# A decode step of attention over a 256 MiB cache: blocks of 8 MiB in three buffers in place of 2 MiB in eight

## The chip, the cores and the metric

The kernel runs on one core of one Trainium2 chip. The metric is device microseconds of one execution. The kernel before has 788.67 us as the median of 3 runs (788.57 to 788.68).

## What is computed

A token each of two sequences goes through grouped-query attention over a cache and, side by side, through a two-layer network. Everything is float32.

```
xn  = layernorm(x)                                   # x: [2, 1, 1024]
q   = (xn @ wq) as [2, 32 heads, 1, 128]             # wq: [1024, 4096]
k,v = k_cache, v_cache                               # each [2, 4 kv heads, 32768, 128]; 8 q heads share one
p   = softmax(q k^T / sqrt(128)) over 32768 positions
a   = (p v) @ wo                                     # wo: [4096, 1024]
m   = silu(xn @ w1) @ w2                             # w1: [1024, 3584], w2: [3584, 1024]
out = x + a + m
```

K and V are 128 MiB each, wq and wo 16 MiB each, w1 and w2 14 MiB each: 316 MiB are read once.

## The kernel before

All large operands come as blocks of 2 MiB, laid out on the host so that each of 128 partitions gets one contiguous row of 16 KiB (`W = 4096` columns). The helper `block` (L35) takes a tile from the pool `stream`, which has 8 buffers (L30), and issues its transfer on SP's queue (L40). SP issues in program order; a transfer into a buffer waits until the last reader of the block that was there has finished. So the order of the blocks in the program is the order of the stream, and up to eight blocks are queued or held.

All matmuls go through the helper `mm` (L44), so the profile gives L44 for each of them and the tile's name tells them apart. TensorE works in four column groups of 32: a matmul with 32 columns of weights writes partitions 32 g to 32 g + 31 of its output. The profile counts two instructions for each matmul.

The program's order is this. `queries(0)` (L108) projects xn with two blocks of wq to the eight queries of kv head 0; `project` (L92) is eight matmuls into `proj`, a copy on ScalarE (L99) and four small products. `mlp_in` (L114) does the same with seven blocks of w1 and keeps silu of the result in `hT`. Then for each kv head h, `queries(h)` for h > 0, `attention(h, b)` for both sequences, and two blocks of wo into the accumulator `acc` (L103). At the end seven blocks of w2 go into `acc`. The last of them is cut: three transfers of 1024 columns (512 KiB, rows of 4 KiB) and four of 256 columns (128 KiB, rows of 1 KiB), so that little work is left behind the last one. ScalarE copies `acc` (L205) and two transfers write the output (L207).

`attention` has two halves. For each of eight K blocks, the scores of 32 query columns (8 heads, the other 24 columns are zero) with 512 positions per column group go to `ps` (a PSUM tile of 128 x 1024, two buffers, L32). VectorE transposes it in 32 x 32 squares to `st` (L140), so that positions lie on partitions and a quarter of the columns is of use, and takes the maximum (L141). After the eighth block the maximum over all partitions is made by two small matmuls (`rm`, `gm`, `gd`, `gmax`, L145 to L155). Then, for each of eight V blocks, VectorE subtracts the maximum (L162), ScalarE takes the exponential (L163), VectorE sums it (`ls`, L164), and eight matmuls with the weights `e` as stationary operand add to `po`. The sum over partitions (`lsum`, L170), its reciprocal and the product with `po` give the head's output in `oT` (L181).

Of the kernel before, what the change touches and what calls it, by code (L numbers as in the profile page):

```python
# [8 lines left out]
F32 = mybir.dt.float32  # L9
AF = mybir.ActivationFunctionType  # L10
# [16 lines left out]
def gqa_plus_mlp_kernel(ctx: ExitStack, tc: tile.TileContext, x, kt, v, wq, wo, w1, w2, out):  # L27
    nc = tc.nc
    const = ctx.enter_context(tc.tile_pool(name="const", bufs=1))
    stream = ctx.enter_context(tc.tile_pool(name="stream", bufs=8))  # L30
    work = ctx.enter_context(tc.tile_pool(name="work", bufs=2))
    ps_s = ctx.enter_context(tc.tile_pool(name="ps_s", bufs=2, space=bass.MemoryType.PSUM))  # L32
    ps_1 = ctx.enter_context(tc.tile_pool(name="ps_1", bufs=1, space=bass.MemoryType.PSUM))

    def block(src, parts=1, first=0):  # L35
        """A streamed block: its first columns in transfers of a row tile, the others in parts."""
        t = stream.tile([P, W], F32, name="blk")
        cuts = [*range(0, first, D), *range(first, W, W // parts), W]
        for lo, hi in zip(cuts, cuts[1:]):
            nc.sync.dma_start(t[:, lo:hi], src[:, lo:hi])  # L40
        return t
# [4 lines left out]
    # ---- constants; sel[p, m] = 1 where p % 32 == m  # L46
    xt = const.tile([B, D], F32, name="xt")
    nc.scalar.dma_start(xt, x)
# [8 lines left out]
    qT = [const.tile([P, B, 32], F32, name=f"qT{i}") for i in range(2)]  # L57
    oT = [const.tile([P, REP, 32], F32, name=f"oT{i}") for i in range(2)]
    hT = const.tile([P, F // P, 32], F32, name="hT")
    xres = const.tile([P, QW], F32, name="xres")  # L60
    for t in (*qT, *oT, hT, xres):
        nc.gpsimd.memset(t, 0.0)
# [18 lines left out]
    xn = const.tile([B, D], F32, name="xn")  # L81
    nc.vector.tensor_scalar(xn, xt, mv[:, 0:1], rstd, op0=ALU.subtract, op1=ALU.mult)
    px = ps_1.tile([P, KT, B], F32, name="small")
    for k in range(KT):
        mm(px[:, k, :], xn[:, k * P:(k + 1) * P], ident[:B, :B])
# [6 lines left out]
    def project(w, o, n):  # L92
# [5 lines left out]
        pr = work.tile([P, 512], F32, name="pr")  # L98
        nc.scalar.copy(pr, pp)  # L99
        for i in range(n):  # L100
            mm(o[:, i, :], pr[:, i * P:(i + 1) * P], sel[:, :B])

    def accumulate(lhsT, w, start, stop):  # L103
        """acc[32 j + b, n] += lhsT[:, b] . w[:, j * 256 + n]"""
        for j in range(4):
            mm(acc[32 * j:32 * j + 32, :], lhsT, w[:, j * QW:(j + 1) * QW], start, stop)

    def queries(h):  # L108
        pq = ps_1.tile([P, REP, B], F32, name="small")
        for n in range(2):  # L110
            project(block(wq[2 * h + n]), pq[:, 4 * n:4 * n + 4, :], 4)
        nc.vector.tensor_copy(qT[h % 2][:, :, :REP], pq.rearrange("p h b -> p b h"))  # L112

    def mlp_in():  # L114
        pre = const.tile([P, F // P, B], F32, name="pre")
        for n in range(N1):
            ph = ps_1.tile([P, 4, B], F32, name="small")
            project(block(w1[n]), ph, 4)
            nc.vector.tensor_copy(pre[:, 4 * n:4 * n + 4, :], ph)
        e = const.tile([P, F // P, B], F32, name="sig")  # L120
        nc.scalar.activation(e, pre, AF.Exp, scale=-1.0)
        nc.vector.tensor_scalar_add(e, e, 1.0)
        r = const.tile([P, F // P, B], F32, name="rsig")
        nc.vector.reciprocal(r, e)
        nc.vector.tensor_mul(hT[:, :, :B], pre, r)

    def attention(h, b):
        q = qT[h % 2][:, b, :]
        # scores, transposed: partition 32 g + i holds positions 512 (4 a + g) + 32 j + i of each block
        s = []  # L130
        mx = work.tile([P, NC, REP], F32, name="mx")
        for c in range(NC):
            kc = block(kt[b, h, c])
            ps = ps_s.tile([P, 1024], F32, name="ps")
            for a in range(2):
                for g in range(4):
                    mm(ps[32 * g:32 * g + 32, a * 512:(a + 1) * 512], q,
                       kc[:, (4 * a + g) * 512:(4 * a + g + 1) * 512])
            st = work.tile([P, 32, 32], F32, name="st", bufs=NC + 1)
            nc.vector.transpose(st.rearrange("p j m -> p (j m)"), ps)  # L140
# [16 lines left out]
        ls = work.tile([P, NC, REP], F32, name="ls")  # L157
        po = ps_1.tile([P, 512], F32, name="po")
        for c in range(NC):
            vc = block(v[b, h, c])  # L160
            e = work.tile([P, 32, REP], F32, name="e", bufs=4)
            nc.vector.tensor_sub(e, s[c][:, :, :REP], gmax.to_broadcast([P, 32, REP]))  # L162
            nc.scalar.activation(e, e, AF.Exp, scale=SCALE)  # L163
            nc.vector.tensor_reduce(ls[:, c, :], e.rearrange("p j m -> p m j"), AX.X, ALU.add)  # L164
# [11 lines left out]
        ob = work.tile([P, 512], F32, name="ob")  # L176
        nc.scalar.copy(ob, po)  # L177
        pt = ps_1.tile([P, REP], F32, name="small")
        for j in range(4):
            mm(pt, ob[:, j * P:(j + 1) * P], sel[:, REP * j:REP * (j + 1)], j == 0, j == 3)  # L180
        nc.vector.tensor_mul(oT[h % 2][:, :, b], pt, rl)  # L181
# [12 lines left out]
    for n in range(N1):  # L194
        last = n == N1 - 1
        w = block(w2[n], 16 if last else 1, first=3 * D if last else 0)
        for i in range(3 if last else 4):
            accumulate(hT[:, 4 * n + i, :], w[:, i * D:(i + 1) * D], False, False)
    f = QW // 4
    for u in range(4):  # L200
        for j in range(4):
            mm(acc[32 * j:32 * j + 32, u * f:(u + 1) * f], hT[:, F // P - 1, :],
               w[:, 3 * D + (4 * u + j) * f:3 * D + (4 * u + j + 1) * f], False, u == 3)
# [33 lines left out]
```

## Time and profile before

| what | us or share |
|---|---|
| median of 3 runs | 788.67 us |
| span of the profiled execution, first to last instruction | 786.9 us |
| mean granted TensorE clock | 0.761 |
| PE busy | 482.1 us, 61% |
| VectorE (DVE) busy | 198.5 us, 25% |
| ScalarE (ACT) busy | 42.2 us, 5% |
| mean rate of the transfers over the span | 422 GB/s |

The page is of one profiled execution. Its rows name the source line, the engine, the operation and the tiles (`out<-in`), then the number of instructions, their busy time, the mean of one, and the idle time of the engine ahead of them with what ended it. "SPq" is the queue on which SP issues transfers, "PEld" the loading of weights into TensorE. In the chain of waits a row is start, length and what ran or was waited for; it is followed back from the last instruction. A transfer's row there runs from its issue to its landing.

### The profile page before, as it was taken

Reading aid. Unit: us, or ns where it says so; the run is one execution under the profiler, and the core shown is the slowest. Engines: PE = TensorE matmul, PEld = TensorE weight load, DVE = VectorE, ACT = ScalarE, POOL = GpSimd, SP = SyncE. Lnnn points to the kernel's source line nnn. Section 1 sums busy time; section 2 is a strip of 40 time slices with the busy share of each in tenths; the row PEclk is TensorE's granted clock in tenths of the full one; section 3 lists DMA queues with packets and bytes.
Section 4 is the critical chain, followed back from the end, with each engine's and each line's share of the span. In section 5 each row is a group of like instructions: output and inputs, shape, how many; then the busy total and the mean of one; then the engine's idle time right before and its main releaser. Section 6 shows DMA issues by size and latency. Waiting matters only on the chain.

```text
span 786.9 us, 7170 instructions
## 1 busy us (share of the span) xinstructions
PE 482.1 (61%) x3048; PEld 139.7 (18%) x3048; DVE 198.5 (25%) x340; ACT 42.2 (5%) x92; POOL 2.4 (0%) x12
## 2 busy tenths in 40 slices
PE   5776666565765566555565565556576565556655
PEld 3331111111221112111221111111131111111122
DVE  2013521342013420443003521352004420333000
ACT  1110000000000000001000000000000010001000
POOL 1000000000000000000000000000000000000000
PEclk9876676868587776978877869776857778857788
DMA  9999999999999999999999999999999999999996
GB/s 375 426 426 428 426 429 426 426 426 426 426 428 427 427 426 427 429 426 425 427 426 427 426 426 426 427 428 428 428 426 424 427 426 428 426 428 429 426 426 273
DMA packets 23682, 331.83 MB, mean 422 GB/s; under 512 B 2642, under 2 KB 3170, under 8 KB 3556
## 3 DMA queue, kind: packets, MB, share of 16 engines
q1 hardware_dynamic: 23624, 331.36, 99.3%
q8 instruction: 24, 0.39, 0.2%
q14 instruction: 6, 0.05, 0.0%
q10 hardware_dynamic: 28, 0.02, 0.0%
HBM read 331.37 MB, written 0.01 MB: 421 GB/s over the span
## 4 chain that ended last, share of the span: by engine, by line
DMA 87%; PE 11%; DVE 1%; issue 0%; ACT 0%; SPq 0%; ACTq 0%
DMA blk<-in_kt 37%; DMA blk<-in_v 33%; DMA blk<-in_w 12%; DMA blk<-in_wq 5%; PE po L44 4%; PE ps L44 3%; PE proj L44 2%; PE small L44 1%; PE acc L44 1%; DVE st L140 0%; SPq L40 0%; ACT pr L99 0%; ACT ob L177 0%; DVE mx L141 0%; DVE e L162 0%
## 5 line engine op out<-in xcount | busy, mean ns | idle before, releaser
L44 PE MATMUL ps<-blk,qT 128*32 128x512 f32 x1024 | 172.1, 805 | 115.0 <-DMA blk<-in_kt 97.7
L44 PE MATMUL po<-blk,e 128*32 128x512 f32 x1024 | 181.0, 849 | 92.5 <-DMA blk<-in_v 82.7
L140 DVE STREAM_TRANSPOSE st<-ps 128x1024 f32<-128x1024 f32 x64 | 80.0, 1250 | 179.5 <-PE ps L44 179.3
L44 PEld LDWEIGHTS ps<-blk,qT 128*32 128x32 f32 x1024 | 37.0, 129 | 241.6 <-issue 147.1
L44 PEld LDWEIGHTS po<-blk,e 128*32 128x32 f32 x1024 | 38.7, 137 | 214.9 <-issue 175.8
L163 ACT ACTIVATE e<-e 128x256 f32<-128x256 f32 x64 | 25.4, 417 | 438.0 <-DVE e L162 438.0
L44 PE MATMUL proj<-blk,xnT 128*32 128x512 f32 x240 | 43.5, 846 | 8.5 <-DMA blk<-in_wq 6.7
L162 DVE TENSOR_TENSOR e<-st,gmax 128x256 f32<-128x256 f32 x64 | 25.7, 422 | 65.2 <-PE po L44 64.7
L164 DVE TENSOR_REDUCE ls<-e 128x8 f32<-128x256 f32 x64 | 38.0, 615 | 13.1 <-ACT e L163 13.0
L181 DVE TENSOR_TENSOR oT<-small,rl 128x8 f32<-128x8 f32 x8 | 1.4, 172 | 157.9 <-PE small L44 157.9
L141 DVE TENSOR_REDUCE mx<-st 128x8 f32<-128x256 f32 x64 | 37.4, 585 | 2.2
L44 PE MATMUL acc<-blk,oT 128*32 128x256 f32 x256 | 25.1, 558 | 10.1 <-DMA blk<-in_wo 9.3
L44 PE MATMUL acc<-blk,hT 128*32 128x256 f32 (+1 forms) x248 | 18.1, 433 | 13.4 <-DMA blk<-in_w 13.2
L44 PE MATMUL small<-sel,pr 128*128 128x2 f32 x120 | 19.1, 281 | 11.0 <-ACT pr L99 11.0
L44 PEld LDWEIGHTS small<-sel,pr 128*128 128x128 f32 x120 | 17.8, 227 | 30.7 <-ACT pr L99 30.7
L112 DVE COPY qT<-small 128x16 f32<-128x16 f32 x4 | 0.7, 174 | 73.1 <-PE small L44 73.1
L44 PE MATMUL small<-ident,rm 128*8 128x128 f32 x16 | 3.5, 306 | 18.2 <-DVE rm L145 18.2
L99 ACT COPY pr<-proj 128x512 f32<-128x512 f32 x15 | 8.8, 585 | 103.2 <-PE proj L44 103.2
L44 PEld LDWEIGHTS acc<-blk,oT 128*32 128x32 f32 x256 | 10.2, 147 | 22.1 <-DMA blk<-in_wo 11.6
L44 PE MATMUL small<-lsum,ones 128*128 128x8 f32 x16 | 3.5, 293 | 15.9 <-DVE lsum L170 15.9
L177 ACT COPY ob<-po 128x512 f32<-128x512 f32 x8 | 4.7, 585 | 156.7 <-PE po L44 156.7
L44 PEld LDWEIGHTS proj<-blk,xnT 128*32 128x32 f32 x240 | 8.5, 135 | 25.6 <-issue 17.1
(49 smaller groups left out, 71.1 us busy)
## 6 DMA issues: line engine op xcount, KB each, us to landing
blk<-in_kt SPq DMA_DIRECT2D x64, 2048.0 KB, 36.2
blk<-in_v SPq DMA_DIRECT2D x64, 2048.0 KB, 36.0
blk<-in_w SPq DMA_DIRECT2D x13, 2048.0 KB, 30.6
blk<-in_wq SPq DMA_DIRECT2D x8, 2048.0 KB, 37.1
blk<-in_wo SPq DMA_DIRECT2D x8, 2048.0 KB, 35.9
blk<-in_w SPq DMA_DIRECT2D x3, 512.0 KB, 30.1
blk<-in_w SPq DMA_DIRECT2D x4, 128.0 KB, 12.4
xres<-in_x ACTq DMA_DIRECT2D x2, 4.0 KB
```

What stands on the lines that cost most here:

```text
L44: nc.tensor.matmul(o, lhsT, rhs, start=start, stop=stop)
L99: nc.scalar.copy(pr, pp)
L112: nc.vector.tensor_copy(qT[h % 2][:, :, :REP], pq.rearrange("p h b -> p b h"))
L140: nc.vector.transpose(st.rearrange("p j m -> p (j m)"), ps)
L141: nc.vector.tensor_reduce(mx[:, c, :], st[:, :, :REP].rearrange("p j m -> p m j"), AX.X, ALU.max)
L162: nc.vector.tensor_sub(e, s[c][:, :, :REP], gmax.to_broadcast([P, 32, REP]))
L163: nc.scalar.activation(e, e, AF.Exp, scale=SCALE)
L164: nc.vector.tensor_reduce(ls[:, c, :], e.rearrange("p j m -> p m j"), AX.X, ALU.add)
L177: nc.scalar.copy(ob, po)
L181: nc.vector.tensor_mul(oT[h % 2][:, :, b], pt, rl)
```

## The change

`W` becomes 16384: a block is 8 MiB, with rows of 64 KiB, and `stream` has three buffers. K and V are two blocks each per head and sequence. The weights are laid out to fit: wq and wo in two blocks of 8 MiB each, w1 and w2 in one of 8 MiB and one of 6 MiB, cut out of rows of 112 KiB. All queries are made at the start, ahead of w1; all of wo is used after the last attention. The helper `block` takes a list of cuts, and the transfers get shorter from the second block of wo on.

On SP's queue the program begins as follows, before the change. `blk` is the streamed tile, `in_w` is w1 here.

```order
L40 DMA blk<-in_wq 128x4096 x2
L40 DMA blk<-in_w 128x4096 x7
L40 DMA blk<-in_kt 128x4096 x8
L40 DMA blk<-in_v 128x4096 x8
L40 DMA blk<-in_kt 128x4096 x8
```

And so after it, where the streamed tiles have names by what they hold.

```order
L43 DMA wqb<-in_wq 128x16384 x2
L43 DMA w1b<-in_w 128x16384
L43 DMA w1b<-in_w 128x12288
L43 DMA kb<-in_kt 128x16384 x2
L43 DMA vb<-in_v 128x16384 x2
```

Four transfers now stand where nine stood, ahead of the first K, with all of wq among them.

The end of SP's queue before, from the last wo on; `in_w` is w2 here.

```order
L40 DMA blk<-in_wo 128x4096 x2
L40 DMA blk<-in_w 128x4096 x6
L40 DMA blk<-in_w 128x1024 x3
L40 DMA blk<-in_w 128x256 x4
L207 DMA out_y<-ot 4x256
```

And after.

```order
L43 DMA wob<-in_wo 128x16384
L43 DMA wob<-in_wo 128x8192 x2
L43 DMA w2b<-in_w 128x8192
L43 DMA w2b<-in_w 128x4096 x3
L43 DMA w2b<-in_w 128x2048 x2
L43 DMA w2b<-in_w 128x1024 x3
L43 DMA w2b<-in_w 128x256 x4
L225 DMA out_y<-ot 4x256
```

The last seven transfers have the sizes they had; the ones ahead of them grow from there backwards.

The scores are packed densely. `qT` holds the eight queries four times, in columns 8 r to 8 r + 7 of a set r that is zero elsewhere. Four matmuls, one for each r, add into one `ps` of 128 x 512, so that each of the four 8-column strips holds other positions. `ps` has four buffers of this size. VectorE then transposes half as wide a tile per 4 MiB as it did per 2 MiB, and all 32 columns of `st` are of use. The weights are made in place in `st`, and `st` itself is the stationary operand of the products with V.

On TensorE one pass of `attention` stands so before. `rm`, `gd` and `lsum` belong to the maximum and the sum, `ob` to the head's output.

```order
L44 MATMUL ps<-blk,qT_83 32x512 x64
L44 MATMUL small<-ident,rm 8x128
L44 MATMUL small<-gd,ones 128x8
L44 MATMUL po<-blk,e 32x512 x32
L44 MATMUL small<-lsum,ones 128x8
L44 MATMUL po<-blk,e 32x512 x32
L44 MATMUL small<-sel,ob 128x8 x4
```

And after.

```order
L47 MATMUL ps<-kb,qT_83 32x512 x64
L47 MATMUL small<-ident,rm 8x128
L47 MATMUL small<-gd,ones 128x8
L47 MATMUL small<-lsum,ones 128x8
L47 MATMUL po<-vb,st 32x512 x64
L47 MATMUL small<-sel,ob 128x8 x4
```

The product with `lsum` has moved from the middle of the products with V to ahead of all of them. `acc`'s matmuls have two columns of weights (`oT` and `hT` hold only the two sequences) in place of 32 with 30 zeros.

The diff, cut to its core:

```diff
-W = 4096                # columns of one streamed block: [128, W] float32, 2 MiB
+W = 16384
+SUB = 4096
...
-    stream = ctx.enter_context(tc.tile_pool(name="stream", bufs=8))
+    stream = ctx.enter_context(tc.tile_pool(name="stream", bufs=3))
...
-    ps_s = ctx.enter_context(tc.tile_pool(name="ps_s", bufs=2, space=bass.MemoryType.PSUM))
+    ps_s = ctx.enter_context(tc.tile_pool(name="ps_s", bufs=4, space=bass.MemoryType.PSUM))
...
-    def block(src, parts=1, first=0):
-        t = stream.tile([P, W], F32, name="blk")
-        cuts = [*range(0, first, D), *range(first, W, W // parts), W]
-        for lo, hi in zip(cuts, cuts[1:]):
+    def block(src, name, cuts=()):
+        t = stream.tile([P, W], F32, name=name, tag="blk")
+        n = src.shape[-1]
+        for lo, hi in zip((0, *cuts), (*cuts, n)):
             nc.sync.dma_start(t[:, lo:hi], src[:, lo:hi])
...
         for c in range(NC):
-            kc = block(kt[b, h, c])
-            ps = ps_s.tile([P, 1024], F32, name="ps")
+            kc = block(kt[b, h, c], "kb")
+            st = work.tile([P, 32, 32], F32, name="st", tag="st", bufs=3)
             for a in range(2):
-                for g in range(4):
-                    mm(ps[32 * g:32 * g + 32, a * 512:(a + 1) * 512], q,
-                       kc[:, (4 * a + g) * 512:(4 * a + g + 1) * 512])
-            st = work.tile([P, 32, 32], F32, name="st", bufs=NC + 1)
-            nc.vector.transpose(st.rearrange("p j m -> p (j m)"), ps)
-            nc.vector.tensor_reduce(mx[:, c, :], st[:, :, :REP].rearrange("p j m -> p m j"), AX.X, ALU.max)
+                ps = ps_s.tile([P, 512], F32, name="ps")
+                for r in range(4):
+                    for g in range(4):
+                        n = (4 * a + g) * 4 + r
+                        mm(ps[32 * g:32 * g + 32, :], qT[h][:, b, r, :], kc[:, n * 512:(n + 1) * 512],
+                           r == 0, r == 3)
+                half = st[:, 16 * a:16 * a + 16, :]
+                nc.vector.transpose(half.rearrange("p j m -> p (j m)"), ps)
+                nc.vector.tensor_reduce(mx[:, 2 * c + a, :], half.rearrange("p j (r m) -> p m (j r)", r=4),
+                                        AX.X, ALU.max)
...
         for c in range(NC):
-            vc = block(v[b, h, c])
-            e = work.tile([P, 32, REP], F32, name="e", bufs=4)
-            nc.vector.tensor_sub(e, s[c][:, :, :REP], gmax.to_broadcast([P, 32, REP]))
-            nc.scalar.activation(e, e, AF.Exp, scale=SCALE)
-            nc.vector.tensor_reduce(ls[:, c, :], e.rearrange("p j m -> p m j"), AX.X, ALU.add)
-            for t in range(8):
-                g = t % 4
-                mm(po[32 * g:32 * g + 32, :], e[:, 4 * t:4 * t + 4, :].rearrange("p j m -> p (j m)"),
-                   vc[:, t * 512:(t + 1) * 512], c == 0 and t < 4, c == NC - 1 and t >= 4)
+            vc = block(v[b, h, c], "vb")
+            for a in range(2):
+                e = s[c][:, 16 * a:16 * a + 16, :]
+                e8 = e.rearrange("p j (r m) -> p (j r) m", r=4)
+                nc.vector.tensor_sub(e8, e8, gmax.to_broadcast([P, 64, REP]))
+                nc.scalar.activation(e, e, AF.Exp, scale=SCALE)
+                nc.vector.tensor_reduce(ls[:, 2 * c + a, :], e8.rearrange("p n m -> p m n"), AX.X, ALU.add)
+                for j in range(16):
+                    g, t = j % 4, 16 * a + j
+                    mm(po[32 * g:32 * g + 32, :], e[:, j, :], vc[:, t * 512:(t + 1) * 512],
+                       c == 0 and t < 4, c == NC - 1 and t >= 28)
...
-    queries(0)
+    for n in range(2):
+        w = block(wq[n], "wqb")
+        for i in range(2):
+            queries(2 * n + i, w[:, 2 * i * SUB:2 * (i + 1) * SUB])
     mlp_in()
     for h in range(HKV):
-        if h:
-            queries(h)
         for b in range(B):
             attention(h, b)
-        for n in range(2):
-            w = block(wo[2 * h + n])
-            for i in range(4):
-                accumulate(oT[h % 2][:, 4 * n + i, :], w[:, i * D:(i + 1) * D], False, False)
-    for n in range(N1):
-        last = n == N1 - 1
-        w = block(w2[n], 16 if last else 1, first=3 * D if last else 0)
-        for i in range(3 if last else 4):
-            accumulate(hT[:, 4 * n + i, :], w[:, i * D:(i + 1) * D], False, False)
+    for n in range(2):
+        w = block(wo[n], "wob", (W // 2,) if n else ())
+        for i in range(16):
+            accumulate(oT[:, 16 * n + i, :], w[:, i * D:(i + 1) * D], False, False)
+    w = block(w2[:, :W], "w2b", (8 * D, 12 * D))
+    for i in range(16):
+        accumulate(hT[:, i, :], w[:, i * D:(i + 1) * D], False, False)
+    lo = 11 * D
+    w = block(w2[:, W:], "w2b", (4 * D, 6 * D, 8 * D, 9 * D, 10 * D, lo, lo + QW, lo + 2 * QW, lo + 3 * QW))
+    for i in range(11):
+        accumulate(hT[:, 16 + i, :], w[:, i * D:(i + 1) * D], False, False)
```

More of the change, by code (lines that the diff above doesn't have):

```diff
@@ L16 @@
 REP = HQ // HKV
-W = 4096
+W = 16384
 NC = SK // W
 KT = D // P
+SUB = 4096
+NQ = HQ * DH // 512
 N1 = F // 512
+FT = F // P
 QW = D // 4
@@ L44, in mm @@
         nc.tensor.matmul(o, lhsT, rhs, start=start, stop=stop)
-    xt = const.tile([B, D], F32, name="xt")
-    nc.scalar.dma_start(xt, x)
+    xt = work.tile([P, D], F32, name="xt", tag="st", bufs=3)
+    nc.scalar.dma_start(xt[:B, :], x)
     ident = const.tile([P, P], F32, name="ident")
@@ L56, in gqa_plus_mlp_kernel @@
     nc.vector.memset(xnT, 0.0)
-    qT = [const.tile([P, B, 32], F32, name=f"qT{i}") for i in range(2)]
-    oT = [const.tile([P, REP, 32], F32, name=f"oT{i}") for i in range(2)]
-    hT = const.tile([P, F // P, 32], F32, name="hT")
+    qT = [const.tile([P, B, 4, 32], F32, name=f"qT{h}") for h in range(HKV)]
+    oT = const.tile([P, HQ, B], F32, name="oT")
+    hT = const.tile([P, FT, B], F32, name="hT")
     xres = const.tile([P, QW], F32, name="xres")
-    for t in (*qT, *oT, hT, xres):
+    for t in (xres, *qT):
         nc.gpsimd.memset(t, 0.0)
@@ L68, in gqa_plus_mlp_kernel @@
     for i in range(2):
-        nc.vector.bn_stats(stats[:, i, :], xt[:, i * 512:(i + 1) * 512])
+        nc.vector.bn_stats(stats[:, i, :], xt[:B, i * 512:(i + 1) * 512])
     mv = const.tile([B, 2], F32, name="mv")
@@ L80, in gqa_plus_mlp_kernel @@
     nc.vector.tensor_mul(rstd, y0, t0)
-    xn = const.tile([B, D], F32, name="xn")
-    nc.vector.tensor_scalar(xn, xt, mv[:, 0:1], rstd, op0=ALU.subtract, op1=ALU.mult)
+    xn = work.tile([P, D], F32, name="xn", tag="st", bufs=3)
+    nc.vector.tensor_scalar(xn[:B, :], xt[:B, :], mv[:, 0:1], rstd, op0=ALU.subtract, op1=ALU.mult)
     px = ps_1.tile([P, KT, B], F32, name="small")
     for k in range(KT):
-        mm(px[:, k, :], xn[:, k * P:(k + 1) * P], ident[:B, :B])
+        mm(px[:, k, :], xn[:B, k * P:(k + 1) * P], ident[:B, :B])
     nc.vector.tensor_copy(xnT[:, :, :B], px)
@@ L90, in gqa_plus_mlp_kernel, with project @@
         mm(acc[32 * j:32 * j + 32, :], ident[:, 32 * j:32 * j + 32], xres, True, False)
-    def project(w, o, n):
+    def project(w, o):
         pp = ps_1.tile([P, 512], F32, name="proj")
@@ L97, in project @@
             mm(pp[32 * g:32 * g + 32, :], xnT[:, k, :], w[:, k * 512:(k + 1) * 512], k < 4, k >= KT - 4)
-        pr = work.tile([P, 512], F32, name="pr")
+        pr = work.tile([P, 512], F32, name="pr", tag="ob")
         nc.scalar.copy(pr, pp)
-        for i in range(n):
+        for i in range(4):
             mm(o[:, i, :], pr[:, i * P:(i + 1) * P], sel[:, :B])
@@ L105, in accumulate, with queries @@
         for j in range(4):
-            mm(acc[32 * j:32 * j + 32, :], lhsT, w[:, j * QW:(j + 1) * QW], start, stop)
-    def queries(h):
+            mm(acc[32 * j:32 * j + B, :], lhsT, w[:, j * QW:(j + 1) * QW], start, stop)
+    def queries(h, w):
         pq = ps_1.tile([P, REP, B], F32, name="small")
         for n in range(2):
-            project(block(wq[2 * h + n]), pq[:, 4 * n:4 * n + 4, :], 4)
-        nc.vector.tensor_copy(qT[h % 2][:, :, :REP], pq.rearrange("p h b -> p b h"))
+            project(w[:, n * SUB:(n + 1) * SUB], pq[:, 4 * n:4 * n + 4, :])
+        for r in range(4):
+            nc.vector.tensor_copy(qT[h][:, :, r, REP * r:REP * (r + 1)], pq.rearrange("p h b -> p b h"))
@@ L114, in mlp_in @@
     def mlp_in():
-        pre = const.tile([P, F // P, B], F32, name="pre")
+        pre = const.tile([P, FT, B], F32, name="pre")
         for n in range(N1):
+            if n % 4 == 0:
+                w = block(w1[:, n * SUB:min(n + 4, N1) * SUB], "w1b")
             ph = ps_1.tile([P, 4, B], F32, name="small")
-            project(block(w1[n]), ph, 4)
+            project(w[:, (n % 4) * SUB:(n % 4 + 1) * SUB], ph)
             nc.vector.tensor_copy(pre[:, 4 * n:4 * n + 4, :], ph)
-        e = const.tile([P, F // P, B], F32, name="sig")
+        e = const.tile([P, FT, B], F32, name="sig")
@@ L121, in mlp_in @@
         nc.scalar.activation(e, pre, AF.Exp, scale=-1.0)
         nc.vector.tensor_scalar_add(e, e, 1.0)
-        r = const.tile([P, F // P, B], F32, name="rsig")
+        r = const.tile([P, FT, B], F32, name="rsig")
         nc.vector.reciprocal(r, e)
-        nc.vector.tensor_mul(hT[:, :, :B], pre, r)
+        nc.vector.tensor_mul(hT, pre, r)
     def attention(h, b):
-        q = qT[h % 2][:, b, :]
         s = []
-        mx = work.tile([P, NC, REP], F32, name="mx")
+        mx = work.tile([P, 2 * NC, REP], F32, name="mx")
@@ L140, in attention @@
-            nc.vector.transpose(st.rearrange("p j m -> p (j m)"), ps)
-            nc.vector.tensor_reduce(mx[:, c, :], st[:, :, :REP].rearrange("p j m -> p m j"), AX.X, ALU.max)
+                ps = ps_s.tile([P, 512], F32, name="ps")
+                for r in range(4):
+                    for g in range(4):
+                        n = (4 * a + g) * 4 + r
+                        mm(ps[32 * g:32 * g + 32, :], qT[h][:, b, r, :], kc[:, n * 512:(n + 1) * 512],
+                           r == 0, r == 3)
@@ L155, in attention @@
         nc.vector.tensor_copy(gmax[:, 0, :], pb)
-        ls = work.tile([P, NC, REP], F32, name="ls")
+        ls = work.tile([P, 2 * NC, REP], F32, name="ls")
         po = ps_1.tile([P, 512], F32, name="po")
         for c in range(NC):
-            vc = block(v[b, h, c])
-            e = work.tile([P, 32, REP], F32, name="e", bufs=4)
-            nc.vector.tensor_sub(e, s[c][:, :, :REP], gmax.to_broadcast([P, 32, REP]))
-            nc.scalar.activation(e, e, AF.Exp, scale=SCALE)
-            nc.vector.tensor_reduce(ls[:, c, :], e.rearrange("p j m -> p m j"), AX.X, ALU.add)
-            for t in range(8):
-                g = t % 4
-                mm(po[32 * g:32 * g + 32, :], e[:, 4 * t:4 * t + 4, :].rearrange("p j m -> p (j m)"),
-                   vc[:, t * 512:(t + 1) * 512], c == 0 and t < 4, c == NC - 1 and t >= 4)
+            vc = block(v[b, h, c], "vb")
[9 more added lines that the diff above has]
+                       c == 0 and t < 4, c == NC - 1 and t >= 28)
         lsum = work.tile([P, REP], F32, name="lsum")
@@ L174, in attention @@
         nc.vector.reciprocal(rl, pl)
-        ob = work.tile([P, 512], F32, name="ob")
+        ob = work.tile([P, 512], F32, name="ob", tag="ob")
         nc.scalar.copy(ob, po)
         pt = ps_1.tile([P, REP], F32, name="small")
-        for j in range(4):
-            mm(pt, ob[:, j * P:(j + 1) * P], sel[:, REP * j:REP * (j + 1)], j == 0, j == 3)
-        nc.vector.tensor_mul(oT[h % 2][:, :, b], pt, rl)
-    queries(0)
+        for r in range(4):
+            mm(pt, ob[:, r * P:(r + 1) * P], sel[:, REP * r:REP * (r + 1)], r == 0, r == 3)
+        nc.vector.tensor_mul(oT[:, REP * h:REP * (h + 1), b], pt, rl)
+    for n in range(2):
+        w = block(wq[n], "wqb")
+        for i in range(2):
+            queries(2 * n + i, w[:, 2 * i * SUB:2 * (i + 1) * SUB])
     mlp_in()
     for h in range(HKV):
-        if h:
-            queries(h)
         for b in range(B):
             attention(h, b)
-        for n in range(2):
-            w = block(wo[2 * h + n])
-            for i in range(4):
-                accumulate(oT[h % 2][:, 4 * n + i, :], w[:, i * D:(i + 1) * D], False, False)
-    for n in range(N1):
-        last = n == N1 - 1
-        w = block(w2[n], 16 if last else 1, first=3 * D if last else 0)
-        for i in range(3 if last else 4):
-            accumulate(hT[:, 4 * n + i, :], w[:, i * D:(i + 1) * D], False, False)
+    for n in range(2):
[9 more added lines that the diff above has]
+        accumulate(hT[:, 16 + i, :], w[:, i * D:(i + 1) * D], False, False)
     f = QW // 4
@@ L201, in gqa_plus_mlp_kernel @@
         for j in range(4):
-            mm(acc[32 * j:32 * j + 32, u * f:(u + 1) * f], hT[:, F // P - 1, :],
-               w[:, 3 * D + (4 * u + j) * f:3 * D + (4 * u + j + 1) * f], False, u == 3)
+            mm(acc[32 * j:32 * j + B, u * f:(u + 1) * f], hT[:, FT - 1, :],
+               w[:, lo + (4 * u + j) * f:lo + (4 * u + j + 1) * f], False, u == 3)
     ot = const.tile([P, QW], F32, name="ot")
@@ L220 @@
         "kt": lay(A_k_cache, (B, HKV, NC, W, DH), (0, 1, 2, 4, 3), (B, HKV, NC, P, W)),
-        "v": lay(A_v_cache, (B, HKV, NC, 2, 4, 16, 32, DH), (0, 1, 2, 4, 6, 3, 5, 7), (B, HKV, NC, P, W)),
-        "wq": lay(A_wq, (KT, P, 2 * HKV, 512), (2, 1, 0, 3), (2 * HKV, P, W)),
-        "wo": lay(A_wo, (2 * HKV, 4, P, D), (0, 2, 1, 3), (2 * HKV, P, W)),
-        "w1": lay(B_w1, (KT, P, N1, 512), (2, 1, 0, 3), (N1, P, W)),
-        "w2": lay(B_w2, (N1, 4, P, D), (0, 2, 1, 3), (N1, P, W)),
+        "v": lay(A_v_cache, (B, HKV, NC, 2, 4, 4, 16, 32, DH), (0, 1, 2, 4, 7, 3, 6, 5, 8), (B, HKV, NC, P, W)),
+        "wq": lay(A_wq, (KT, P, 2, 4, 512), (2, 1, 3, 0, 4), (2, P, W)),
+        "wo": lay(A_wo, (2, 16, P, D), (0, 2, 1, 3), (2, P, W)),
+        "w1": lay(B_w1, (KT, P, N1, 512), (1, 2, 0, 3), (P, N1 * SUB)),
+        "w2": lay(B_w2, (FT, P, D), (1, 0, 2), (P, FT * D)),
     }
-    last = arrays["w2"][-1, :, 3 * D:]
+    last = arrays["w2"][:, -D:]
     last[:] = lay(last, (P, 4, 4, QW // 4), (0, 2, 1, 3), (P, D))
-    nc = bacc.Bacc("TRN2", target_bir_lowering=False, num_devices=1)
+    nc = bacc.Bacc("TRN2", target_bir_lowering=False, num_devices=1, dynamic_dma_scratch_size=2048)
     args = [nc.dram_tensor(f"in_{k}", a.shape, mybir.dt.from_np(a.dtype), kind="ExternalInput").ap()
```

## The prediction

> **What bounds it now.** I read the page's slices and its DMA queues first, because a kernel that reads 316 MiB once may simply be a stream. The first row is the rate in 40 slices of 19.67 us, the next three are the queues (packets, MB, share of the 16 engines' time), the last the chain that ended last, by engine.
>
> ```profile
> GB/s 375 426 426 428 426 429 426 426 426 426 426 428 427 427 426 427 429 426 425 427 426 427 426 426 426 427 428 428 428 426 424 427 426 428 426 428 429 426 426 273
> q1 hardware_dynamic: 23624, 331.36, 99.3%
> q8 instruction: 24, 0.39, 0.2%
> q14 instruction: 6, 0.05, 0.0%
> DMA 87%; PE 11%; DVE 1%; issue 0%; ACT 0%; SPq 0%; ACTq 0%
> ```
>
> There is no dip between the first slice and the last: q1, SP's queue, fills 99.3% of the 16 engines' time, and the chain that ended last is 87% transfers. TensorE, at 61% busy, only waits. So the time is the stream's own time, the start before it and the tail behind it, and a change acts through one of three doors: how fast the stream runs, whether it ever runs dry, and how long the end is.
>
> How is the stream made up? These are the issues, with count and size.
>
> ```profile
> blk<-in_kt SPq DMA_DIRECT2D x64, 2048.0 KB, 36.2
> blk<-in_v SPq DMA_DIRECT2D x64, 2048.0 KB, 36.0
> blk<-in_w SPq DMA_DIRECT2D x13, 2048.0 KB, 30.6
> blk<-in_wq SPq DMA_DIRECT2D x8, 2048.0 KB, 37.1
> blk<-in_wo SPq DMA_DIRECT2D x8, 2048.0 KB, 35.9
> blk<-in_w SPq DMA_DIRECT2D x3, 512.0 KB, 30.1
> blk<-in_w SPq DMA_DIRECT2D x4, 128.0 KB, 12.4
> ```
>
> That is 164 transfers of 128 rows. 164 x 128 rows are 20,992 packets; q1 has 23,624, which is 16 more for each transfer (2,624) and 8 for the output. So one row of 16 KiB travels as one packet, and each of the 16 engines carries 8 rows and one closing packet per transfer.
>
> **What a row costs beyond its bytes.** Three sizes are on the trace. For 2 MiB I take the chain of waits between 457 and 537 us (start, length, what), where the stream waits for nothing; for the small ones the timeline of the end (start, length, engine, and in brackets the idle time and what ended it).
>
> ```profile
> 420.57 37.12 DMA blk<-in_v
> ...
> 459.80 37.12 DMA blk<-in_kt
> ...
> 499.02 37.11 DMA blk<-in_v
> ```
>
> ```profile
> 780.52 0.16 PEld L44 LDWEIGHTS acc<-blk,hT 128*32 128x32 f32 x8 [0.62 <-DMA blk<-in_w]
> 781.82 0.16 PEld L44 LDWEIGHTS acc<-blk,hT 128*32 128x32 f32 x8 [1.14 <-DMA blk<-in_w]
> ...
> 782.91 0.16 PEld L44 LDWEIGHTS acc<-blk,hT 128*32 128x32 f32 x8 [0.19 <-DMA blk<-in_w]
> 783.26 0.16 PEld L44 LDWEIGHTS acc<-blk,hT 128*32 128x32 f32 x8 [0.19 <-DMA blk<-in_w]
> 783.64 0.37 ACT L205 COPY ot<-acc 128x256 f32<-128x256 f32 x1 [40.84 <-PE acc L44]
> ```
>
> The chain's landings are at 457.69, 496.92 and 536.13, 8 transfers apart: 39.22 / 8 = 4.9025 us per 2 MiB. In the tail two 512 KiB transfers land 781.82 - 780.52 = 1.30 us apart, and two of 128 KiB 783.26 - 782.91 = 0.35 us. Write the time of a transfer as a + b x MiB. From 2 MiB and 512 KiB, 3a = 4 x 1.30 - 4.9025, so a = 0.099 us and b = 2.40 us per MiB; the reading error of 0.01 us in 1.30 makes a 0.086 to 0.113. With that b the 128 KiB transfer gives a = 0.35 - 0.30 = 0.05. So each transfer of 128 rows loses 0.05 to 0.11 us beside its bytes. I take 0.09: the pair of longer rows is the nearer one, and I stay at the low side of its reading error because the shorter row points down.
>
> A figure of the Trainium skill speaks to this (DMA: Bandwidth & Descriptors, Where 436 GB/s comes from): the ports' ceiling is 435.2 GB/s. By it 2 MiB cannot take less than an estimated 4.819 us, a is at most 0.084, and the sum below would be 9.4 us in place of 10.1; no slice here is over 429, so the trace agrees with the ceiling and cannot test it at long rows.
>
> **The stream, counted.** After the change SP issues 52 transfers of 128 rows: two of wq, two of w1, 32 of K and V, and 16 at the end (1 + 2 of wo, 13 of w2, by the order shown above). The bytes are the same. 164 - 52 = 112 transfers fewer, at 0.09 us: **-10.1 us**; with 0.05 it is -5.6, with 0.113 it is -12.7. It all lies on the path, since nothing covers a stream that is the path.
>
> **The end** stays. The last seven transfers are again three with 4 KiB rows and four with 1 KiB rows; TensorE's last group of eight starts at 783.26 on the last landing, and ScalarE's copy follows at 783.64. The cuts ahead of them are 8 KiB rows or longer, and their transfers are in the 52. What the matmuls into 2 rows instead of 32 save, at most a part of a weight load of 0.16 us, I set at nothing, with that as its bound.
>
> The instruction fetches (q8, q14) ride on the same engines: 24 of 16 KiB stay, as the matmuls are the same in number; the 6 small ones may become fewer with VectorE's 287 rows becoming 175. 0.05 of 331.8 MB is 0.1 us: nothing.
>
> **Does the stream run dry with three buffers?** A block's buffer is free when TensorE has read it last; the two behind it keep the queue full for 2 x 19.34 = 38.7 us (8 x 2.406 + 0.09). TensorE's time for 2 MiB of K comes in two sizes, by the granted clock; the first two rows are from the chain of waits. The others are the price of VectorE's groups, and the chain from the last scores to the first product with V.
>
> ```profile
> 413.60 3.68 PE ps L44 x16
> ...
> 497.05 1.96 PE ps L44 x16
> ```
>
> ```profile
> L140 DVE STREAM_TRANSPOSE st<-ps 128x1024 f32<-128x1024 f32 x64 | 80.0, 1250 | 179.5 <-PE ps L44 179.3
> L162 DVE TENSOR_TENSOR e<-st,gmax 128x256 f32<-128x256 f32 x64 | 25.7, 422 | 65.2 <-PE po L44 64.7
> L164 DVE TENSOR_REDUCE ls<-e 128x8 f32<-128x256 f32 x64 | 38.0, 615 | 13.1 <-ACT e L163 13.0
> ```
>
> ```profile
> 703.31 0.02 issue
> ...
> 708.59 8.26 PE po L44 x48
> ```
>
> At the slow size all along, 8 MiB take 4 x 3.68 = 14.7 us. The new order adds one wait: the product with `lsum` now stands ahead of all products with V on TensorE, so that those wait until VectorE and ScalarE have made the weights of both V blocks. Packing leaves the useful scores as many as before, so this is as much as eight blocks take today, 8 x (0.422 + 0.615) = 8.3 us. From the last K landing, the first V block is then free after at most 14.7 + 5.3 (703.31 to 708.59) + 8.3 + 14.7 = 43.0 us; the queue would be dry three blocks after that landing, at 58.0. Covered by 15 us. Over a whole pass TensorE and what it waits for need at most 4 x 14.7 + 5.3 + 8.3 = 72.4 us against 4 x 19.34 = 77.4 of stream, which leaves 5.0 for the output's few small products. The dense packing takes three quarters of the 80.0 us of transposes off VectorE; it waited 179.3 us for TensorE there, so this is worth nothing now.
>
> The front is narrower. There are 15 projections in a row at the start now, and no K between them. Their price at the slow clock is on the chain of waits, and at the fast one on the timeline.
>
> ```profile
> 3.56 30.65 DMA blk<-in_w
> ...
> 39.88 3.61 PE proj L44 x16
> ...
> 46.07 3.26 PE proj L44 x16
> ```
>
> ```profile
> 16.40 1.92 PE L44 MATMUL proj<-blk,xnT 128*32 128x512 f32 x16
> ...
> 20.01 1.92 PE L44 MATMUL proj<-blk,xnT 128*32 128x512 f32 x16
> ```
>
> That is 6.19 us or 3.61 us each, so a block of four takes 24.8 or 14.4. The first of these rows is SP's sixth transfer: 12 MiB had landed at 3.56 + 30.65 = 34.2, so 8 MiB land at 34.2 - 9.8 = 24.4, the next at 43.7 and 63.1, w1's 6 MiB at 77.6 and the first K at 96.9. At the fast clock every buffer is free more than 15 us early. At the slow clock throughout, the buffers come free at 49.2, 74.0 and 98.8; the last one is 1.9 us late. My value is no stall, as the granted clock alternates; the bound is in the second rival.
>
> **Sum.** Span 786.9 - 10.1 = 776.8; the median of the runs, 788.67, lies 1.8 above the span, and that does not change. **778.6 us.** A measurement here tells 0.2% (1.6 us) from no change; its three runs differ by 0.11.
>
> **Rivals.** *Bytes alone set the pace, or a long row travels as several packets of 16 KiB.* Then the 0.09 us per 128 rows stay, and the time is 788.4 to 788.7. For it: no row of this trace is longer than 16 KiB. Against it: the rate rises with the row, from 128 KiB / 0.35 us = 374 GB/s over 512 KiB / 1.30 us = 403 to 428, and 16 KiB rows are whole packets. Chance 0.09.
>
> *The front runs dry.* At the slow clock for the first 100 us the second K block is issued 1.9 us late, and a stream that starts afresh loses more: the first slice has 375 against 426 GB/s, 12% of 19.67 us, 2.4 us. Together 4.3 us: 782.9. For it: the chain from 34 to 53 us is projections at the slow clock. Against it: the first two after 16 us ran fast. Chance 0.07.
>
> *The stream gets slower with long rows.* The engines read from addresses that lie four times as far apart as before, and memory could serve them in a worse pattern. The mechanism sits in all 36 transfers with rows of 64 KiB, 288 MiB. Each 1% of 428 GB/s is 288 x 2.45 x 0.01 = 7.1 us; it decides from 1.4% on, where it eats the 10.1. If it takes 2% more than the gain, slower by 14 us: 803. If it takes 1% more, 795.8, which is the price I give. Against it: nothing on the trace slows with row length, and slices differ by no more than 424 to 429. The Trainium skill has such a rule (DMA: Bandwidth & Descriptors, Latency and other measured facts): copies slow down when the rows of the 128 partitions lie a large power of two apart, 207 of 214 GB/s at 512 KiB and half at 4 MiB. By it 64 KiB should still be near full rate; no run here shows it yet. Chance 0.10.
>
> **Numbers.** Forecast 0.74, the others 0.09, 0.07 and 0.10. Range: low end from a = 0.113 (788.67 - 12.7 = 776.0, and 0.2 for the fetches and weight loads), high end from a = 0.05 (783.1), which takes in the front (782.9) with 0.4 to spare: 775.8 to 783.5 holds 0.81. Faster 0.82 (forecast, front, and a share of a partial gain), same 0.09, slower 0.09.
>
> **What would show it.** q1 with 52 x 128 + 52 x 16 + 8 = 7,496 packets; slices at 431 to 436 GB/s; about 19.3 us between two landings of 8 MiB; no dip in the slices near 96 us; 3.6 us from the last landing to the end. A count of packets near 23,000, or slices still at 427, means the first rival; a dip the second; slices below 426 the third. I am wrong most of all if something in rows of 64 KiB behaves otherwise than the line through 4 and 16 KiB.

## The result and the profile after

The changed kernel takes 776.6 us (median of 4 runs, 776.52 to 776.83), against 788.67 before: a ratio of 0.9847, 95% interval 0.9833 to 0.9861. It is faster by 12.1 us; 10.1 were forecast, and 776.6 lies in the range. The profiled execution has 776.54 us and a span of 774.8.

These are the slices of the page after, q1's packets, and the chain by engine.

```profile
GB/s 387 434 436 434 437 430 444 443 434 433 431 433 431 431 433 431 433 441 433 434 433 434 433 434 433 437 434 430 434 433 431 433 431 433 431 433 421 431 429 281
q1 hardware_dynamic: 7496, 331.36, 99.0%
DMA 68%; PE 22%; DVE 7%; ACT 1%; issue 1%; another core or an unknown queue 0%; SPq 0%; ACTq 0%
```

The packets are the 7,496 foreseen, so a row of 64 KiB is one packet. From the second slice to the 36th the rate is 430 to 444 where it was 424 to 429, with no dip at 96 us; one of 421 stands near the end. The chain has 22% of TensorE where it had 11%. That is no sign of a slower TensorE, which is busy for 402.6 us here and was for 482.1: with three buffers the transfer that lands last was issued when a product ended, so the chain now runs through the release of buffers. One pass shows it (start, length, what).

```profile
379.08 47.27 DMA kb<-in_kt
...
426.48 9.77 PE ps L47 x64
...
448.31 9.08 PE po L47 x64
457.40 46.15 DMA kb<-in_kt
...
503.69 8.72 PE ps L47 x64
```

46 us for a block of 19.3 means that it lay 27 us behind others in the queue: the stream never saw the release. The last K blocks of two passes land at 379.08 + 47.27 = 426.35 and 457.40 + 46.15 = 503.55, four blocks apart: 19.30 us for 8 MiB, against 4 x 4.9025 = 19.61 before. That is 434.6 GB/s. The single slices above 436 are no rate that lasts: by the packets no block of 8 MiB lands less than 19.3 us behind the one ahead of it.

The end, on TensorE's weight loads and ScalarE.

```profile
768.49 0.11 PEld L47 LDWEIGHTS acc<-w2b,hT 128*2 128x2 f32 x8 [0.88 <-DMA w2b<-in_w]
769.74 0.11 PEld L47 LDWEIGHTS acc<-w2b,hT 128*2 128x2 f32 x8 [1.15 <-DMA w2b<-in_w]
...
771.11 0.11 PEld L47 LDWEIGHTS acc<-w2b,hT 128*2 128x2 f32 x8 [0.22 <-DMA w2b<-in_w]
771.47 0.37 ACT L223 COPY ot<-acc 128x256 f32<-128x256 f32 x1 [63.90 <-PE acc L47]
```

From the last landing to the end of the span there are 3.7 us, as foreseen. But the two transfers of 512 KiB land 1.25 us apart, where it was 1.30, with the same rows of 4 KiB. Nothing in the prediction says that a row which the change leaves alone gets faster. That was the first loose thread.

### The profile page after: what moved, and what is told of

It reads as the page before. It is cut to its first block, busy times and chain, and to the rows that moved or that the text cites. A ratio compares the mean times of both kernels' runs of the same rounds, so it can differ in the third digit from the quotient of the medians.

```text
span 774.8 us, 6628 instructions
## 1 busy us (share of the span) xinstructions
PE 402.6 (52%) x3048; PEld 131.6 (17%) x3048; DVE 129.0 (17%) x224; ACT 36.4 (5%) x60; POOL 2.0 (0%) x11
## 3 DMA queue, kind: packets, MB, share of 16 engines
q1 hardware_dynamic: 7496, 331.36, 99.0%
## 4 chain that ended last, share of the span: by engine, by line
DMA 68%; PE 22%; DVE 7%; ACT 1%; issue 1%; another core or an unknown queue 0%; SPq 0%; ACTq 0%
DMA kb<-in_kt 48%; PE ps L47 9%; DMA w2b<-in_w 8%; PE po L47 8%; DMA vb<-in_v 6%; DMA wqb<-in_wq 5%; DVE ls L178 3%; PE proj L47 2%; PE small L47 2%; DVE st L176 2%; DVE mx L152 1%; DVE st L151 1%; ACT pr L103 1%; ACT st L177 0%
## 5 line engine op out<-in xcount | busy, mean ns | idle before, releaser
L47 PE MATMUL ps<-kb,qT 128*32 128x512 f32 x1024 | 146.1, 734 | 145.3 <-DMA kb<-in_kt 145.3
L47 PE MATMUL po<-vb,st 128*32 128x512 f32 x1024 | 145.7, 733 | 71.8 <-DMA vb<-in_v 71.8
L47 PEld LDWEIGHTS ps<-kb,qT 128*32 128x32 f32 x1024 | 39.9, 132 | 244.9 <-issue 233.9
L47 PEld LDWEIGHTS po<-vb,st 128*32 128x32 f32 x1024 | 37.6, 131 | 172.8 <-issue 172.6
L151 DVE STREAM_TRANSPOSE st<-ps 128x512 f32<-128x512 f32 x32 | 22.9, 717 | 244.7 <-PE ps L47 244.7
L177 ACT ACTIVATE st<-st 128x512 f32<-128x512 f32 x32 | 19.5, 630 | 359.2 <-DVE st L176 359.0
L152 DVE TENSOR_REDUCE mx<-st 128x8 f32<-128x512 f32 x32 | 34.8, 1087 | 1.1
L178 DVE TENSOR_REDUCE ls<-st 128x8 f32<-128x512 f32 x32 | 32.6, 1061 | 5.6 <-ACT st L177 5.6
L47 PE MATMUL acc<-wob,oT 128*2 128x256 f32 x256 | 19.2, 470 | 15.5 <-DMA wob<-in_wo 15.5
L176 DVE TENSOR_TENSOR st<-st,gmax 128x512 f32<-128x512 f32 x32 | 20.6, 685 | 0.3
```

The source lines that it names most:

```text
L47: nc.tensor.matmul(o, lhsT, rhs, start=start, stop=stop)
L151: nc.vector.transpose(half.rearrange("p j m -> p (j m)"), ps)
L152: nc.vector.tensor_reduce(mx[:, 2 * c + a, :], half.rearrange("p j (r m) -> p m (j r)", r=4), AX.X, ALU.max)
L176: nc.vector.tensor_sub(e8, e8, gmax.to_broadcast([P, 64, REP]))
L178: nc.vector.tensor_reduce(ls[:, 2 * c + a, :], e8.rearrange("p n m -> p m n"), AX.X, ALU.add)
```

## The experiments

The theory to begin with was the prediction's: 128 rows and their transfer lose about 0.10 us beside their bytes (0.09 then; 0.10 from the 19.30 above), and the change has 112 transfers fewer. The rival was that the gain comes from the packing, the order or the rest of the change. All times are medians; the kernel before took 788.6 to 788.7 beside them.

### The changed kernel with rows of 16 KiB

```diff
     def block(src, name, cuts=()):
...
+        cuts = cuts or range(4096, n, 4096)
         for lo, hi in zip((0, *cuts), (*cuts, n)):
```

> The changed kernel, with each block of 8 MiB fetched by four transfers of 4096 columns (rows of 16 KiB, 2 MiB each), as before the change; buffers, packing, order and the end stay as changed. 110 transfers and four times the rows more than the changed kernel (776.6 us). Theory (0.10 us is lost for every 128 rows beside their bytes): 110 x 0.10 = 11.0, so 787.6 us, between 786.8 and 788.2. Rival (the gain came from the packing, the order of the work or fewer instruction fetches): 776.6 to 778.

Measured: 781.3 us (781.22 to 781.37). Neither. Four times the rows cost 4.7 us, 0.043 for each of 110 transfers, less than half of what the theory asks, and the other 7.3 us of the gain are still there with the rows and the transfers of before. By the packets there are two transfers fewer than the 23,624 packets of before stand for, and yet the stream is faster.

```profile
q1 hardware_dynamic: 23336, 331.36, 99.5%
```

```profile
100.00:700.00 600.00, 362.06 (x2084) 90.14 (x2080) 119.40 (x181) 23.66 (x39) 0.00 (x0) 0.78 1.01 431
```

This row is the stretch from 100 to 700 us: busy time of the five engines, granted clock, DMA share, and at its end GB/s. It says 431, where the kernel before has this:

```profile
100.00:700.00 600.00, 361.88 (x2190) 96.55 (x2186) 161.14 (x261) 27.87 (x64) 0.00 (x0) 0.76 1.01 427
```

### Rows of 32 KiB

```diff
+        cuts = cuts or range(8192, n, 8192)
```

> The same with two transfers of 8192 columns (rows of 32 KiB, 4 MiB each) for a block. Theory, linear in the number of rows: 37 transfers more at 0.10, 780.3 us. Rival (a threshold at 16 KiB, or something that only a full 64 KiB row does): 776.6, or all of the loss, 787.6.

Measured: 778.09 us. Linear it is, 1.5 us for 37 transfers, 0.040 each; but at the smaller price.

### One transfer with rows of 16 KiB

```diff
+    def block4(src, name):
+        t = stream.tile([P, W], F32, name=name, tag="blk")
+        nc.sync.dma_start(t.rearrange("p (g m) -> p g m", g=4), src.rearrange("g p m -> p g m"))
+        return t
...
-            kc = block(kt[b, h, c], "kb")
+            kc = block4(kt[b, h, c], "kb")          # and V; [4, 128, 4096] in memory
```

> The changed kernel, with the blocks of K and V laid out as four pieces of 128 x 4096 one behind the other, and fetched by one transfer of 8 MiB with 512 rows of 16 KiB. The number of transfers is that of the changed kernel, the rows are those of before. If the loss belongs to the row (the packet), 32 blocks x 3 x 0.09 to 0.10 = 8.6 to 9.6 more: 785.2 to 786.2 us. If it belongs to the transfer (its issue and its closing packet), 776.6.

Measured: 780.25 us, 3.65 more than the changed kernel. Each of the 16 engines gets 32 x 24 = 768 packets more, so a row costs 4.8 ns by itself, 0.038 us for the eight rows that an engine has in a transfer.

### More transfers with whole rows

```diff
+        if not cuts and n == W:
+            for g in range(4):
+                nc.sync.dma_start(t[g::4, :], src[g::4, :])
+            return t
```

> The changed kernel, with each block of 8 MiB fetched by four transfers of 32 partitions (every fourth), with whole rows of 64 KiB. The rows are those of the changed kernel, the transfers are 108 more. If the loss belongs to the row: 776.6 to 777.7 us (the closing packets alone, 108 x 9 ns). If it belongs to the transfer: 108 x 0.10 = 10.8 more, 787.4. Above 790 the choice of partitions would have brought a cost of its own.

Measured: 778.2 us, 1.6 for 108 transfers, 0.015 each; 0.5 above the range for the row alone. The loss belongs mostly to the rows. The two prices, 0.038 and 0.015, sum to 0.053, while the first run gave 0.043 for both: they do not quite add up.

So the first theory had a cause and the wrong price, and 7 us were without an owner. The same rows of 16 KiB, in 2 MiB transfers, land every 4.90 us before and every 4.86 in the first experiment. What differs between the two for a row that is being carried? Not the distance of the rows in memory: the run with one transfer has that of before, and its packets of 16 KiB take as long as those of the first experiment (612.1 and 612.6 ns on average, by the packets in the traces), where the kernel before has 617.3. I looked up where the buffers lie. Before, they start at byte 35872 of a partition and every 16384 from there, which is 32 past a multiple of 64 (and of 256). After, they start at 11776, a multiple of 512. The sizes of what is allocated ahead of them add up to both. The new theory: a row whose destination starts off a boundary costs more, about 0.040 us per 128 rows. The rival is still the rest of the change.

### The kernel before, with its buffers moved

```diff
+    pad = const.tile([P, 56], F32, name="pad")      # 224 bytes; buffers now at 36096, 52480, ...
+    nc.vector.memset(pad, 0.0)
```

> The kernel before, with one unused tile of 224 bytes a partition allocated ahead of the streamed buffers, so that they start at multiples of 256 bytes (36096, 52480 ...) in place of 32 bytes past a multiple of 64 (35872, 52256 ...). Nothing else differs. Theory (the buffers' start costs the rows of the kernel before 0.040 us per transfer of 2 MiB: 4.901 there against 4.861 in the run with 16 KiB rows in the changed kernel): 157 x 0.040 = 6.3 less than 788.6, 782.3 us, between 781.5 and 783. Rival (packing, order or the number of buffers made that difference): 788.6.

Measured: 781.91 us, ratio 0.9915 (0.990 to 0.993). 224 unused bytes are worth 6.8 us. The chain of waits has the price per transfer.

```profile
416.78 36.79 DMA blk<-in_v
...
455.68 36.79 DMA blk<-in_kt
...
494.58 36.79 DMA blk<-in_v
```

Landings at 453.57, 492.47 and 531.37: 38.90 us for 16 MiB, 4.8625 per transfer where it was 4.9025. The rate of the same stretch:

```profile
100.00:700.00 600.00, 360.95 (x2201) 94.21 (x2193) 164.22 (x267) 27.99 (x65) 0.00 (x0) 0.77 1.01 431
```

The packets show it one by one: those of 16 KiB take 612.8 ns on average here, 4.5 less than the 617.3 of the kernel before.

### The 16 KiB rows, moved off the boundary

```diff
+    pad = const.tile([P, 8], F32, name="pad")       # 32 bytes; buffers at 11808, ...
+    nc.vector.memset(pad, 0.0)
```

> The changed kernel with four transfers of 16 KiB rows for a block (781.3 us), and an unused tile of 32 bytes ahead of the buffers, so that they start 32 bytes past a multiple of 512, as they do, modulo 64, in the kernel before. Theory: 149 transfers of 2 MiB at 0.040 more, 787.3 us. Rival: 781.3.

Measured: 788.24 us (10 runs, 788.12 to 788.5), 6.9 more. With rows and offset put back, the kernel stands 0.5 from the one before: the packing, the order, the three buffers and the finer end are together worth about that, or nothing, since the interval of the ratio (0.9984 to 1.0003) takes in no difference. Packets of 16 KiB are back at 617.2 ns. The chain gives 530.96 and 570.18, 39.22 us for 16 MiB, as before.

```profile
491.75 39.21 DMA vb<-in_v
530.98 39.20 DMA kb<-in_kt
```

### The changed kernel, moved off the boundary

The same 32 bytes in the changed kernel.

> The changed kernel itself (776.6 us) with its buffers moved by 32 bytes in the same way. If the offset costs a fixed time for each row, 52 transfers of 128 rows at 0.040 more: 778.7 us. If it costs a share of the bytes (0.8%): 782.9. Rival (no cost of the offset): 776.6.

Measured: 778.9 us (778.86 to 779.02). A fixed time for each row, then, 2.3 us for 52 transfers, 0.044 each, and packets of 64 KiB take 2,426.9 ns where they took 2,422.7, 4.2 more, much like the 4.5 of the short ones; long rows pay it as seldom as they pay the other one. The two transfers of 512 KiB land 1.29 us apart again.

```profile
770.60 0.11 PEld L47 LDWEIGHTS acc<-w2b,hT 128*2 128x2 f32 x8 [0.76 <-DMA w2b<-in_w]
771.89 0.11 PEld L47 LDWEIGHTS acc<-w2b,hT 128*2 128x2 f32 x8 [1.19 <-DMA w2b<-in_w]
```

### 64 bytes off

The same with 16 columns, 64 bytes.

> The same as the run with 16 KiB rows and 32 bytes of offset, but with 64 bytes of offset. If a start at any multiple of 64 bytes is as good as one at 512: 781.3 us. If the boundary that counts is larger: up to 787.3.

Measured: 786.85 us, 5.5 of the 6.9, or 0.034 for each of the 162 transfers. A start 64 bytes past a multiple of 256 is nearly as bad as one 32 past it; a multiple of 256 (the moved kernel before) is enough. 128 was not tried.

The Trainium skill has a rule that comes near (DMA: Bandwidth & Descriptors, How a descriptor splits into AXI transactions): what a transfer reads in one go must begin at a multiple of 256 bytes, and a start off that boundary makes the first piece reach back and fetch bytes it does not use. The runs agree with the 256, but the page speaks of reading, and here the start that moved is the destination's. Its two examples add one beat for a start 32 bytes off and seven for one 224 off, and a beat is an estimated 1.2 ns at the 850 MHz of that page; counted in the same way, a row 64 bytes off would add an estimated two beats, more than one 32 bytes off, and the run lost less. So the size, 0.040 us for 8 rows on an engine, 5 ns a row, is the measurement's, and why the boundary costs that much stays open.

### Two buffers

```diff
-    stream = ctx.enter_context(tc.tile_pool(name="stream", bufs=3))
+    stream = ctx.enter_context(tc.tile_pool(name="stream", bufs=2))
```

> The changed kernel with two streamed buffers in place of three. Theory (the queue needs only one block of 19.3 us ahead while the other is read): after the last K landing of a pass the first V block is free at 31 us (21.8 to its first product and 9.1 for its products, on the profile of the changed kernel), the queue would be dry at 38.6; so it holds at the mean clock, and loses a few us in a pass whose products run at the slow clock: 776.6 to 784, most likely 779. Rival (a block must wait in the queue besides the one that lands and the one in use): 36 blocks lose a fresh start of about 2 us each, 850.

Measured: 785.3 us (781.3 to 785.6), 1.3 above the range, and the place is another one. The profiled execution is the one of 781.3 us, 4.7 above the changed kernel. In it the passes lose nothing, the front does: from 60 to 80 us, while the projections with w1 run, the stream falls to 374 GB/s, where the changed kernel has 437 (two rows of this run, then one of the changed kernel). The passes, in the last row, run at 433 as with three buffers. What the slower executions lose beyond that, about 4 us, no profile shows.

```profile
0.00:60.00 60.00, 35.09 (x204) 16.47 (x208) 5.29 (x26) 5.59 (x9) 1.97 (x11) 0.91 0.99 418
60.00:80.00 20.00, 15.37 (x120) 7.01 (x116) 1.08 (x8) 2.93 (x5) 0.00 (x0) 0.91 0.93 374
```

```profile
60.00:80.00 20.00, 14.20 (x104) 6.09 (x108) 0.71 (x5) 2.34 (x4) 0.00 (x0) 0.83 1.01 437
```

```profile
100.00:700.00 600.00, 300.31 (x2088) 89.50 (x2088) 121.09 (x183) 23.65 (x39) 0.00 (x0) 0.74 1.00 433
```

### The end, cut as little as before

```diff
-        w = block(wo[n], "wob", (W // 2,) if n else ())
+        w = block(wo[n], "wob", ())
...
-    w = block(w2[:, :W], "w2b", (8 * D, 12 * D))
+    w = block(w2[:, :W], "w2b")
...
-    w = block(w2[:, W:], "w2b", (4 * D, 6 * D, 8 * D, 9 * D, 10 * D, lo, lo + QW, lo + 2 * QW, lo + 3 * QW))
+    w = block(w2[:, W:], "w2b", (8 * D, 9 * D, 10 * D, lo, lo + QW, lo + 2 * QW, lo + 3 * QW))
```

> The changed kernel with the end cut as little as before the change: the second block of wo and the first of w2 whole, the second of w2 as one piece of 4 MiB, three of 512 KiB and four of 128 KiB. 47 transfers in place of 52. Theory: 5 x 0.04 less, 776.4 us, if TensorE catches up; at the slow clock it may be up to 4 us late at the end. Rival (the growing pieces hide work at the end): 778 to 780.

Measured: 776.67 us, no different from the change. The pieces that grow backwards from the end neither cost nor gain.

### The end, not cut

```diff
+    w = block(w2[:, W:], "w2b", ())                 # and the two above
```

> The changed kernel with no cut at all at the end: the last 6 MiB of w2 are one transfer, and all their 48 products come after its landing. Theory: 96 instructions at 1.91 us per 32, the first 32 at 3.50 (the slow clock), 7.3 in place of 0.4, less 15 transfers at 0.04: about 783 us. Rival (the end is hidden anyway): 776.

Measured: 783.7 us, 7.1 more. All the last products stand behind the last landing, in one row of the timeline. They are 120 instructions where 96 were expected, since the last 1,024 columns are used in 16 products of a quarter of the size, and the transfers are 12 fewer, not 15.

```profile
770.84 7.24 PE L47 MATMUL acc<-w2b,hT 128*2 128x256 f32 x120 [5.11 <-DMA w2b<-in_w]
```

### Rows 512 KiB apart

```diff
-        "kt": lay(A_k_cache, (B, HKV, NC, W, DH), (0, 1, 2, 4, 3), (B, HKV, NC, P, W)),
+        "kt": lay(A_k_cache, (B, HKV, NC, W, DH), (0, 4, 1, 2, 3), (B, P, HKV, NC, W)),
...
-            kc = block(kt[b, h, c], "kb")
+            kc = block(kt[b, :, h, c, :], "kb")     # V in the same way
```

> The changed kernel with K and V laid out in memory so that the rows of the 128 partitions lie 512 KiB apart in place of 64 KiB; the rows of 64 KiB, the transfers and all else stay. Theory (the distance of the rows plays no part, as 16 KiB rows took the same 611 ns at a distance of 64 KiB and of 16 KiB): 776.6 us. Rival (the third of the prediction): 3% of 32 x 19.3 us more, 795.

Here the rows of V lie in another order than the weights, so its sums are others than the reference's; bytes, transfers and work are the same. Measured: 776.83 us, 0.2 from the change, and the same rate: the first row is this run's, the second the changed kernel's. Packets of 64 KiB take 2,423.2 ns, against 2,422.7.

```profile
100.00:700.00 600.00, 298.78 (x2077) 89.49 (x2073) 121.18 (x183) 23.65 (x39) 0.00 (x0) 0.73 1.00 433
```

```profile
100.00:700.00 600.00, 299.99 (x2088) 89.24 (x2084) 121.09 (x183) 23.64 (x39) 0.00 (x0) 0.74 1.00 433
```

The rule of the Trainium skill that the third rival leaned on (DMA: Bandwidth & Descriptors, Latency and other measured facts), 207 of 214 GB/s at 512 KiB, does not show in loads with rows of 64 KiB; the page measured copies with rows of 16 KiB from memory to memory.

## Why the prediction was right, point by point

**A stream that is the path.** Right. The rate rose and the time fell by as much; TensorE's 79.5 us and VectorE's 69.5 us less of busy time are nowhere in the result.

**0.09 us per transfer of 128 rows.** Right for the kernel on which it was read, and short of a part of the change that I did not see. Four runs beside the two kernels part it; all have the same bytes.

| | buffers 32 bytes off | buffers on the boundary |
|---|---|---|
| rows of 16 KiB, the kernel before | 788.7 | 781.9 |
| rows of 16 KiB, the changed kernel | 788.2 | 781.3 |
| rows of 64 KiB, the changed kernel | 778.9 | 776.6 |

Down the left column the change is worth 9.8 us, where the prediction has 10.1, and 778.9 is its 778.6; 9.3 of it are the longer rows (788.2 to 778.9), 0.085 for each of 110 transfers. My line through 2 MiB and 512 KiB was drawn through transfers that all paid for the offset, and a cost by row is just what such a line finds. Through the ones on the boundary, 4.8625 and 1.25 us, it gives (4 x 1.25 - 4.8625) / 3 = 0.046. The step that failed is the one behind it: "112 transfers fewer, at 0.09 us" let the other 52 keep their price. They lost 0.044 each as well, 2.3 us, because the tiles ahead of the buffers, which the change resized, happen to end on a multiple of 512. 9.8 + 2.3 is the 12.1 measured. The prediction's second sum, 9.4, has the same gap: it holds for the rows with the offset (9.3), not for the whole. That the time still lies in the range is in part luck: the low end was drawn for an error of reading, and a gain with another cause fell into it. Of the 0.09, about half is the row and its transfer (0.043), half the offset.

Put the other way: on the boundary, the whole change is worth 5.3 us (781.9 to 776.6), the long rows 4.7 of it, and most of the gain, 6.8 us, was open to the kernel before for 224 bytes.

One count in the prediction is off without weight: by the pages VectorE has 340 instructions before and 224 after, not 287 and 175. The small fetches on q14 went from 6 to 4, and the term is nothing as it was set.

**The end stays.** Right: 3.6 foreseen, 3.7 found. The two runs on it show that the last seven small transfers are worth the 7 us, and the new pieces ahead of them nothing.

**Three buffers do not run dry.** Right. The wait for `lsum` is there: from the last K landing at 426.35 to the first product with V at 448.31 pass 22.0 us, under the bound of 28.3, and the first V block is free at 457.40, 31.1 after the landing, where the bound was 43.0 and the queue dry at 58.0. The front is the narrow place, as the second rival had it: with two buffers it is there that the stream stalls in the execution profiled.

**The rivals.** A row as several packets: no, 7,496. The front: not with three buffers. A slower stream: no, not even with eight times the distance.

What stays open: the price of rows and that of transfers, measured apart, sum to 0.053 and together give 0.043. The packets themselves take 611, 1,213 and 2,418 ns (medians, on the boundary) for 16, 32 and 64 KiB, which is 8.7 ns a row beside its bytes, more than the 4.8 that the time shows; but eight of 612.6 and a closing one of 9 add up to 4.91 us where transfers land every 4.86, so they overlap. Also open are 128 bytes of offset, and why the boundary costs what it does.

## What to carry to other kernels

When a stream of transfers is the path, look where its buffers start before changing its shape: a pad of less than 256 bytes is the cheapest experiment there is, and any change of a pool's size makes it by accident. Longer rows pay too, by a fixed time for each row saved, up to the 64 KiB tried here. And a price read off a trace holds under that trace's conditions: ask which of them the change moves without saying so.

## What the runs showed of the hardware

A row whose destination starts 32 bytes past a multiple of 256 costs about 5 ns more on its engine (0.040 us per 128 rows), whether it has 16 or 64 KiB; 64 bytes past it, with rows of 16 KiB, about 4 ns (0.034 us). A row by itself costs 4.8 ns beside its bytes in the time of the kernel, a further transfer 15 ns. In the stretch from 100 to 700 us that makes 427, 431 and 433 GB/s for the kernel before, the same moved, and the changed one. The distance of rows in memory made no difference: packets of 16 KiB take 611 ns (median) at 16 and at 64 KiB, packets of 64 KiB take 2,418 at 64 and at 512 KiB.
